# Expert 0's first tile from one-hot products, the index behind it, and what is moved around them

## The chip, the core and the metric

One core of a Trainium2 chip runs one program. The metric is the device time of one execution in microseconds (us); the kernel before took 702.99 us (median of 3 runs, 701.35 to 705.62). Engines: PE (TensorE, matmul), with PEld for its weight loads; DVE (VectorE); ACT (ScalarE); POOL (GpSimd); SP (SyncE, which here only issues DMAs). A trailing q, as in ACTq, is the engine's queue: it issues DMAs and reads registers, in order with the engine's own work.

## The reference

Three stages follow one another; each needs all of the one before.

```python
# 1. attention: 4 batches x 8 heads, 576 positions, head size 64, causal window of 64
scores = q @ k.T / 8, masked to 0 <= i - j < 64; attn = softmax(scores); o = attn @ v
x = o as 2304 tokens x 512
# 2. routed experts: 8 experts, 512 -> 1024 -> 512
do_compute = x @ w_skip > 0                      # the other tokens pass through
e = argmax(x @ w_gate); gate = softmax(x @ w_gate)[e]
x[do_compute] += gate * (relu(x @ w1[e]) @ w2[e])
# 3. dense: 512 -> 2048 -> 512
h = x @ w_in; g = h where h >= 1, 0 where h <= -1, else (h + 1)**2 / 4; out = g @ w_out
```

## The kernel before

All in float32, or in pairs of reduced-precision halves (`split`, L130, and `split_pair`, L134: ACT writes the high half, DVE or POOL the rest). The order on every engine is the order of the text; the framework adds only the waits.

**Attention** (L274 to L696) runs over 18 tiles of 128 tokens (NT = 18), software-pipelined: in iteration t come the value product of tile t-3 (`stage_v`), the transposes of t-2 (`stage_t`), the scores of t (`stage_s`), the logits of earlier tiles (`stage_x`, `stage_l`, `stage_l2`) and the routing. Before the first scores, 69 bf16 matmuls (`warm`, L584) run on a constant. Meanwhile SP loads q, k and v and, through `load_raws` (L101), raw expert weights of 512 KB each into 6 buffers, of which `most[0]` may be in use.

**Routing** takes groups of 3 tiles (ROUTES): `route_a` finds each token's expert, `route_b` its rank among that expert's tokens (running counts by matmul), `route_h` makes two one-hot tables and `route_c` multiplies them into a list of token numbers by expert and slot: `acc` for the groups so far, `idx` at the end. `route_g` stores the gates. Groups begin at tiles 0, 3, ..., 15; the last two at t0 = 12 and t1 = 15. Each x tile is stored to the DRAM table `x1` (`store_t`), its gate in column 512.

**Experts** (L699 to L886): expert 0's first tile is gathered from `x1` by `idx` (`fetch(0, 0)`, an indirect DMA issued by POOL), transposed on PE and split (`pre`, `prep`); then `ffn` runs ha, hb, their transposes, and y. `values_load...` (L833) reads the counts of tokens into registers on every engine, ahead of expert 0. Between `fetch(0, 0)` and `pre(0, 0)` stand two weight splits, ACT then DVE; DVE waits in front of its share (`tick_seen`, L824) until POOL has issued the gather. After them ACT issues up to four raw loads (L829). A tile has 128 tokens: experts 2 and 4 have a second one in this run, expert 4 a third, whose gather `fetch(e, 2)` is issued at L866. Within `ffn`, `hooks` place splits, conversions of stage 3's weights (`turn`) and the next expert's preparation.

**Dense stage** (L889 to L1107): 18 tiles in 6 blocks, PE back to back.

`keep_warm(n)` issues n matmuls on constants whose result nobody reads; 14, 20, 80 and 6 of them stand in the end of attention.

Of the kernel before, what the change touches and what calls it, by code (L numbers as in the profile page):

```python
# [13 lines left out]
I32 = mybir.dt.int32  # L14
# [43 lines left out]
WARM = 69  # L58
WARM_COLUMNS = 108
# [3 lines left out]
KEEP = (14, 20, 80, 6, 36)  # L63
PASSES = ((0, 0), (0, 1), (1, 0))
PX_END = {3: "s2", 2: "s1", 1: "s0"}
# [4 lines left out]
def moe_chain(  # L70
# [200 lines left out]
    rawp.append(mctx.enter_context(tc.tile_pool(name="raw1", bufs=RAWS[1])))  # L271


    with ExitStack() as actx:  # L274
# [10 lines left out]
        nc.gpsimd.memset(zero, 0.0)  # L285
        wg_sb = ldp.tile([P, KD, WGW], F32, tag="wg", name="wg_sb", bufs=1)
# [4 lines left out]
        qt = {}  # L291

# [16 lines left out]
        misc = psp.tile([P, 512], F32, tag="misc", name="misc")  # L309
# [10 lines left out]
        def stage_s(t):  # L320


            i, b0 = divmod(2 * t, B)
            m = none if i == 0 else odd if i % 2 else even
            e, o = (i, i - 1) if i % 2 == 0 else (i - 1, i)
            e, o = place[e % 4], place[o % 4]
            s = [psp.tile([P, 4, P], F32, tag=f"s{(2 * t + k) % 3}", name=f"s{2 * t + k}") for k in range(2)]
# [26 lines left out]
        def stage_t(t):  # L354
            last = t + 1 == NT
            if last:
                both = ldp.tile([P, 2, 4, P], F32, tag="q", name="pts_last")
            for k in range(2):
                g = 2 * t + k
                pr = st.pop(("p", g))  # L360
                pt = psp.tile([P, 4, P], F32, tag=f"s{k}" if last else f"pt{k}", name=f"pt{g}")
                for p in range(4):
                    nc.tensor.transpose(pt[:, p, :], pr[:, p, :], ident)
                pts = both[:, k] if last else ap2.tile([P, 4, P], F32, tag="pts", name=f"pts{g}")

                if last or k == 0 or t + 3 == NT:
                    nc.scalar.activation(pts, pt, AF.Copy)
                else:
                    nc.vector.tensor_copy(pts, pt)
                st["pt", g] = pts  # L370

        def stage_v(t):
# [9 lines left out]
            x = ap2.tile([P, H, D], F32, tag="x", name=f"x{t}", bufs=3)  # L382
# [14 lines left out]
            st["x", t] = x.rearrange("p h d -> p (h d)")  # L397
            i, b = divmod(2 * t, B)
# [6 lines left out]
        def stage_x(t):  # L405
            x = st.pop(("x", t))
            px = psp.tile([P, KD, P], F32, tag=PX_END.get(NT - t, f"s{(2 * t + 2) % 3}"), name=f"px{t}")
# [14 lines left out]
        def stage_l(t):  # L422
# [11 lines left out]
            ls = sm.tile([P, P], F32, tag="ls", name=f"ls{t}", bufs=2)  # L434
# [5 lines left out]

        def keep_warm(n):
            spare = psp.tile([P, P], F32, tag="o", name="spare")
            for _ in range(n):
                nc.tensor.matmul(spare, lhsT=ones, rhs=ones, start=True, stop=True)
# [33 lines left out]
        def route_b(t, n, side):  # L478
# [21 lines left out]
            if t + 2 * n < NT:  # L500
                for i in range(n):
                    nc.gpsimd.tensor_tensor(run, run, oh[:, i], ALU.add)
            elif t + n == NT:
                cn = end["rk"][:, 1, 0 : NE + 1]
                for i in range(n):
                    nc.tensor.matmul(cn, lhsT=ones, rhs=oh[:, i], start=(i == 0), stop=False)
                for i in range(n):
                    nc.tensor.matmul(cn, lhsT=ones, rhs=st["oh", t - n][:, i], start=False, stop=False)
                nc.tensor.matmul(cn, lhsT=ones, rhs=run, start=False, stop=True)
                keep_warm(KEEP[1])  # L510
# [3 lines left out]
            nc.vector.tensor_reduce(ps, r2, axis=AX.X, op=ALU.add)  # L514
            rc = sm.tile([P, 2, n], F32, tag="rc", name=f"rc{t}")
# [7 lines left out]
            if t + n == NT:  # L523
                st["cn"] = cn
# [12 lines left out]
        def route_h(t, n, tiles=None):  # L537

            rc = st["rc", t]
            for i in range(n) if tiles is None else tiles:  # L540

                if t + n == NT:
                    eng, also = dve if i == n - 1 else pool, dve
                else:
                    eng = also = dve if t + 2 * n >= NT and i == n - 1 else pool
# [9 lines left out]
        def route_c(t, n):  # L555
# [4 lines left out]
            near = t + 2 * n < NT <= t + 3 * n  # L560
            mid = t + n < NT <= t + 2 * n
            for i in reversed(range(n)):
                to, at = st.pop(("to", t + i))
                nc.tensor.matmul(
                    ix, lhsT=to, rhs=at, start=(not last and not mid and i == n - 1),
                    stop=(not near and not mid and i == 0),
                )
            if last:
                keep_warm(KEEP[2])
            if not near and not mid:  # L570
# [27 lines left out]
        of = {}  # L598
        for j, n in enumerate(ROUTES):
            t0 = len(of)  # L600
            of.update({t0 + i: (t0, i, n, j % 2) for i in range(n)})
        due, since, gates = {}, {}, {}
        for t in range(NT - 1):
# [9 lines left out]
            most[0] = 1 if t < 3 else 2 if t + 4 < NT else RAWS[0] + RAWS[1]  # L613
# [9 lines left out]
            if t >= 5:  # L623
                t0, i, n, side = of[t - 5]
                if i == n - 1:
                    route_a(t0, n)
                    for f, l in (
                        (partial(route_b, t0, n, side), 1),
                        (partial(route_h, t0, n), 1),
                        (partial(route_c, t0, n), 3),  # L630
                    ):
                        due.setdefault(t + l, []).append(f)
                    gates[t + 1] = partial(route_g, t0, n)
# [11 lines left out]
        t1, n = NT - ROUTES[-1], ROUTES[-1]  # L645
        t0 = t1 - ROUTES[-2]
        ranks, later = due.pop(NT - 1), [f for g in sorted(due) for f in due[g]]
        stage_v(NT - 4)
        stage_t(NT - 3)
        stage_s(NT - 1)  # L650
        store_t(NT - 4, nc.sync)
        stage_l2(NT - 6, *of[NT - 6][1:])
        stage_l(NT - 5)
        stage_x(NT - 4)
        stage_v(NT - 3)
        store_t(NT - 3, nc.sync)
        stage_t(NT - 2)
        stage_t(NT - 1)
        ranks[0]()
        stage_v(NT - 2)  # L660
        store_t(NT - 2, nc.sync)
        for f in ranks[1:]:
            f()
        stage_v(NT - 1)
        store_t(NT - 1, nc.sync)
        stage_x(NT - 3)
# [5 lines left out]
        route_a(t0, of[t0][2])  # L672
        end["lg"] = psp.tile([P, 4, P], F32, tag="pt1", name="lg_end")[:, 0, 0 : n * (NE + 1)]
        for f in gates.values():
            f()
# [3 lines left out]
        route_b(t0, *of[t0][2:])  # L679
        route_h(t0, of[t0][2], range(n - 1))  # L680
# [3 lines left out]
        keep_warm(KEEP[3])  # L684
        stage_l2(NT - 1, *of[NT - 1][1:])
        route_g(t0, of[t0][2])
        for f in later:
            f()
# [10 lines left out]
    with ExitStack() as ectx:  # L699
# [3 lines left out]
        def bank(i, shape, name):  # L703
            return psp.tile(shape, F32, tag=f"bank{i}", name=name)
# [25 lines left out]
        def prep(x, name, tag="mxT", into=None):  # L730
            px = bank(3 if tag == "mxT" else 7, [P, KD, P], f"mpx{name}")
            for c in range(KD):
                nc.tensor.transpose(px[:, c, :], x[:, c * P : (c + 1) * P], ident)
# [86 lines left out]
        early_pool.append(ectx.enter_context(tc.tile_pool(name="earlier", bufs=len(EARLY) // 2)))  # L820
        fetch(0, 0)
# [4 lines left out]
        pre(0, 0)  # L826
# [4 lines left out]
        for e in range(1, AHEAD):  # L831
# [3 lines left out]
        for e in range(NE):  # L835
# [9 lines left out]
            def second():  # L845

                xeT[e, 1] = mp.tile([P, 2, KD, P], F32R, tag="mxT", name=f"mxT{e}_1")
                with tc.If(counts[e] > P):
                    prep(xe[e, 1], f"{e}_1", "mxTl", xeT[e, 1])

# [4 lines left out]
                    work(turn if e else [], [dve]),  # L855
# [9 lines left out]
            with tc.If(counts[e] > P):  # L865
                fetch(e, 2)  # L866
# [22 lines left out]
    with ExitStack() as fctx:  # L889
# [153 lines left out]
        keep_warm(KEEP[4])  # L1043
# [121 lines left out]
```

## Time and profile before

| | us |
|---|---|
| median of 3 runs | 702.99 |
| the profiled execution | 703.17 |
| its span, first to last instruction | 701.5 |
| attention, to the last value product | 0 to about 97.6 |
| routing of the last tiles, first gather | about 97.6 to 116.5 |
| experts | 116.5 to about 271 |
| dense stage | about 271 to 701.5 |

The span is 1.67 us shorter than the execution's time; that part lies around the program. The prediction is made against 703.17. A time such as "at 103.77" is counted from the span's start. In lines of the timeline the first number is the start, the second the length, "x12" a count of instructions merged into one line, and the bracket at the end tells how long the engine was idle before and what ended that.

### The profile page before, as it was taken

Reading aid. Unit: us, or ns where it says so; the run is one execution under the profiler, and the core shown is the slowest. Engines: PE = TensorE matmul, PEld = TensorE weight load, DVE = VectorE, ACT = ScalarE, POOL = GpSimd, SP = SyncE. Lnnn points to the kernel's source line nnn. Section 1 sums busy time; section 2 is a strip of 40 time slices with the busy share of each in tenths; the row PEclk is TensorE's granted clock in tenths of the full one; section 3 lists DMA queues with packets and bytes.
Section 4 is the critical chain, followed back from the end, with each engine's and each line's share of the span. In section 5 each row is a group of like instructions: output and inputs, shape, how many; then the busy total and the mean of one; then the engine's idle time right before and its main releaser. Section 6 shows DMA issues by size and latency. Waiting matters only on the chain.

```text
span 701.5 us, 12250 instructions
## 1 busy us (share of the span) xinstructions
PE 674.2 (96%) x4630; PEld 575.6 (82%) x4630; DVE 425.6 (61%) x808; ACT 385.9 (55%) x768; POOL 90.7 (13%) x137
## 2 busy tenths in 40 slices
PE   7999989999998998999999999999999999999997
PEld 6777778776776765987989999999999999999995
DVE  4888864897781799787888854444433433433332
ACT  5887742583751764566766655454444454445443
POOL 3255545222210221000000000000000000000000
PEclk9999998999999999999999999999999999999999
DMA  8999953897891693442333202121300030001001
GB/s 259 288 272 290 307 133 115 289 329 275 267 357 31 205 332 95 172 127 84 121 92 96 69 0 61 31 60 31 91 1 0 1 91 0 1 1 45 1 1 45
DMA packets 34504, 88.83 MB, mean 127 GB/s; under 512 B 6958, under 2 KB 8110, under 8 KB 34420
## 3 DMA queue, kind: packets, MB, share of 16 engines
q1 hardware_dynamic: 26208, 73.82, 34.3%
q10 hardware_dynamic: 5892, 7.35, 3.1%
q0 software_dynamic: 2320, 6.58, 2.8%
q8 instruction: 48, 0.79, 0.5%
q14 instruction: 36, 0.29, 0.1%
HBM read 75.65 MB, written 13.12 MB: 127 GB/s over the span
## 4 chain that ended last, share of the span: by engine, by line
PE 55%; DVE 3%; ACT 1%; issue 1%; ACTq 0%; DVEq 0%
PE h L922 27%; PE po L950 26%; PE spare L1038 1%; PE p2x L912 1%; DVE c L943 1%; DVE c L940 1%; ACT q L933 1%; DVE w L137 1%; DVE gs L941 0%; DVE q L932 0%; DVE x2T L132 0%; ACT q L929 0%; DVE q L936 0%; ACT part L959 0%; ACT w L136 0%
## 5 line engine op out<-in xcount | busy, mean ns | idle before, releaser
L922 PE MATMUL h<-x2T,w 128*128 128x384 f32 x1152 | 218.0, 337 | 1.1 <-DVE x2T L132 0.9
L950 PE MATMUL po<-w,gs 128*128 128x512 f32 x864 | 217.3, 395 | 1.7 <-ACT w L136 0.9
L922 PEld LDWEIGHTS h<-x2T,w 128*128 128x128 f32 x1152 | 204.6, 188 | 10.0 <-DVE x2T L132 1.7
L950 PEld LDWEIGHTS po<-w,gs 128*128 128x128 f32 x864 | 159.5, 188 | 32.3 <-ACT w L136 1.2
L929 ACT ACTIVATE q<-h 128x384 f32<-128x384 f32 x96 | 47.0, 489 | 108.1 <-PE h L922 104.2
L932 DVE TENSOR_SCALAR q<-q 128x384 f32<-128x384 f32 x96 | 34.4, 358 | 98.2 <-ACT q L929 98.0
L936 DVE TENSOR_TENSOR q<-hs,q 128x384 f32<-128x384 f32 x96 | 53.7, 559 | 49.8 <-ACT q L933 49.8
L938 ACT ACTIVATE gs<-q 128x384 fp32r<-128x384 f32 x96 | 50.4, 525 | 60.0 <-DVE q L936 60.0
L941 DVE TENSOR_TENSOR gs<-q,gs 128x384 fp32r<-128x384 f32 x96 | 53.6, 559 | 44.4 <-ACT gs L938 44.4
L136 ACT ACTIVATE w<-raw 128x1024 fp32r<-128x1024 f32 x64 | 65.3, 1056 | 18.7 <-PEq L869 4.7
L798 PE MATMUL y<-w,hT 128*128 128x512 f32 x264 | 70.2, 403 | 4.1 <-DVE hT L132 2.8
L137 DVE TENSOR_TENSOR w<-raw,w 128x1024 fp32r<-128x1024 f32 x55 | 64.8, 1219 | 3.8 <-ACT w L136 1.9
L933 ACT ACTIVATE q<-q 128x384 f32<-128x384 f32 x96 | 50.5, 526 | 22.2 <-DVE q L932 18.6
L798 PEld LDWEIGHTS y<-w,hT 128*128 128x128 f32 x264 | 47.3, 188 | 17.3 <-DVE hT L132 4.5
L349 ACT ACTIVATE pr<-s,nb 128x128 f32<-128x128 f32 x144 | 39.2, 384 | 16.5 <-DVE nb L345 16.5
L931 ACT ACTIVATE hs<-h 128x384 f32<-128x384 f32 x96 | 46.7, 487 | 0.0
L759 PE MATMUL ha<-w,mxT 128*128 128x512 f32 x132 | 35.3, 416 | 3.7 <-ACT mxT L131 1.5
L759 PEld LDWEIGHTS ha<-w,mxT 128*128 128x128 f32 x132 | 25.1, 197 | 13.2 <-issue 4.5
L759 PE MATMUL hb<-w,mxT 128*128 128x512 f32 x132 | 35.2, 402 | 0.0
L345 DVE TENSOR_REDUCE nb<-s 128x4 f32<-128x512 f32 x36 | 23.2, 686 | 16.0 <-PE s L338 14.5
L724 POOL DMA_INDIRECT x<-mx,idx x11 | 16.5, 1501 | 115.6 <-POOLq L865 60.4
L131 ACT ACTIVATE hT<-hTp 128x512 fp32r<-128x512 f32 x22 | 13.2, 599 | 27.1 <-PE hTp L772 13.0
(170 smaller groups left out, 702.1 us busy)
## 6 DMA issues: line engine op xcount, KB each, us to landing
raw<-in_wu SPq DMA_DIRECT2D x61, 512.0 KB, 6.0
raw<-in_wd SPq DMA_DIRECT2D x31, 512.0 KB, 4.0
x<-x SPq DMA_DIRECT2D x22, 256.0 KB, 3.2
vt<-in_vs SPq DMA_DIRECT2D x36, 130.0 KB, 6.2
out<-out SPq DMA_DIRECT2D x36, 128.0 KB, 2.4
x<-x ACTq DMA_DIRECT2D x17, 256.0 KB, 6.6
q<-in_qs SPq DMA_DIRECT2D x8, 512.0 KB, 5.0
kt<-in_ks SPq DMA_DIRECT2D x8, 512.0 KB, 6.2
```

Of the source, the lines that this page charges most:

```text
L136: nc.scalar.activation(t[:, 0], src, AF.Copy)
L137: eng.tensor_tensor(t[:, 1], src, t[:, 0].bitcast(F32), ALU.subtract)
L759: nc.tensor.matmul(ph, lhsT=xT[:, a, c, :], rhs=halves[4 * e + j, c][:, b, :], start=(n == 0), stop=(n == len(seq) - 1),)
L798: nc.tensor.matmul(py, lhsT=hT[j][:, a, c, :], rhs=halves[4 * e + 2 + j, c][:, b, :], start=(j == 0 and n == 0), stop=(j == 1 and n == len ...
L922: nc.tensor.matmul(ph, lhsT=halves[U_IN + m // 4, c][:, b, (m % 4) * P : (m % 4 + 1) * P], rhs=xT[:, a, c, :], start=(n == 0), stop=(n == ...
L929: nc.scalar.activation(q, ph, AF.Relu, bias=0.5, scale=0.5)
L931: nc.scalar.activation(h, ph, AF.Copy)
L933: nc.scalar.activation(q, q, AF.Square)
L936: nc.vector.tensor_tensor(q, h, q, ALU.max)
L938: nc.scalar.activation(gs[:, 0], q, AF.Copy)
L941: dve.tensor_tensor(gs[:, 1], q, gs[:, 0].bitcast(F32), ALU.subtract)
L950: nc.tensor.matmul(po[i], lhsT=gs[:, a, i * P : (i + 1) * P], rhs=w[:, b, :], start=(m == m0 and (a, b) == PASSES[0]), stop=(m == m1 - 1 a ...
```

## The change

- The 69 matmuls at the start become 6: float32, 512 columns, on a tile `warmer` that DVE fills with ones after its other constants.
- The four `keep_warm` calls in the end of attention go.
- At most 2 raw buffers are filled at t = 14 (6 before), 3 at t = 15 and 16, and 6 from a new `load_raws()` on, behind `stage_v(NT - 3)`.
- x of tiles 12 to 17 stays in SBUF (`xs_late`; 12 to 14 in parts of k's buffer that are no longer used).
- The group of tiles 9 to 11 is ranked earlier and added to `acc`; `gather_ahead` then fetches the rows of expert 0's first tile that lie in tiles 0 to 11 into `rows`, which POOL has cleared.
- `choose` makes for each late tile a one-hot matrix from rank to slot (tiles 12 to 14 by two activations on ACT, 15 to 17 by one operation on DVE), and `add_rows` multiplies the tile with it: six tiles and `rows` (against the identity) add up in PSUM to the transposed tile that `prep` splits.
- `route_h` and `route_c` of the last groups, so `idx` and `cnt_i`, come behind these products; the gates of the last two groups behind `route_a`, those of tiles 9 to 11 much earlier.
- The gathers of expert 1 and then expert 0 are issued ahead of `tick_seen`; those behind it are expert 0's second tile and expert 2's first.
- `fetch(e, 2)` moves into the middle of the expert's first tile (it stood behind that tile's store).
- An expert that has one conversion in `turn` does it in hook 2, not in hook "a".

```diff
-WARM = 69
-WARM_COLUMNS = 108
+WARM = 6
-KEEP = (14, 20, 80, 6, 36)
+KEEP = 36
...
+        warmer = ap2.tile([P, 4, P], F32, tag="pr", name="warmer", bufs=4)
+        nc.vector.memset(warmer, 1.0)
...
+        def choose(t, i, eng):
+            sel = kept(*SEL_AT[t + i - t0], P)
+            ps = st["ps", t][:, i : i + 1]
+            if eng is nc.scalar:
+                off = sm.tile([P, P], F32, tag="ls", name=f"off{t + i}", bufs=3)
+                nc.scalar.activation(off, slot_r[:, 0], AF.Abs, bias=ps)
+                nc.scalar.activation(sel, off, AF.Relu, bias=1.0, scale=-1.0)
+            else:
+                eng.tensor_scalar(sel, slot_r[:, 0], ps, 0.0, op0=ALU.add, op1=ALU.is_equal)
+            return sel
+        def gather_ahead():
+            at = sm.tile([P, 1], I32, tag="ahead", name="ahead", bufs=1)
+            nc.vector.tensor_copy(at, acc[:, 0:1])
+            nc.gpsimd.indirect_dma_start(
+                out=rows, out_offset=None, in_=x1[0 : t0 * P], in_offset=bass.IndirectOffsetOnAxis(ap=at, axis=0),
+                bounds_check=t0 * P - 1, oob_is_err=False,
+            )
+        def add_rows(px, x, sel, first=False, last=False):
+            for c in range(KD):
+                nc.tensor.matmul(
+                    px[:, c, :], lhsT=x[:, c * P : (c + 1) * P], rhs=sel,
+                    start=(first and c == 0), stop=(last and c == KD - 1),
+                )
...
-        warm = psp.tile([P, P], F32, tag="o", name="warm")
+        warm = psp.tile([P, H, P], F32, tag="o", name="warm")[:, 0:4]
         for _ in range(WARM):
-            nc.tensor.matmul(warm[:, 0:WARM_COLUMNS], lhsT=ones, rhs=ones[:, 0:WARM_COLUMNS], start=True, stop=True)
+            nc.tensor.matmul(warm, lhsT=warmer[:, 0], rhs=warmer, start=True, stop=True)
...
-            most[0] = 1 if t < 3 else 2 if t + 4 < NT else RAWS[0] + RAWS[1]
+            most[0] = 1 if t < 3 else 2 if t + 3 < NT else 3
...
+        x0 = bank("s0", "mpx0_0")
+        sels = [choose(t0, 0, nc.scalar)]
+        add_rows(x0, xs_late[t0], sels[0], first=True)
         route_a(t1, n)
-        route_h(t0, of[t0][2], [n - 1])
+        route_p(t0, n0)
+        route_h(t0, n0, range(n0 - 1))
+        sels += [choose(t0, i, nc.scalar) for i in range(1, n0)]
+        route_g(t0, n0)
         route_g(t1, n)
-        keep_warm(KEEP[0])
         route_b(t1, *of[t1][2:])
-        route_h(t1, n)
-        route_c(t0, of[t0][2])
+        for i in range(1, n0):
+            add_rows(x0, xs_late[t0 + i], sels[i])
+        add_rows(x0, rows, ident)
+        sels += [choose(t1, i, dve) for i in range(n)]
+        for i in range(n):
+            add_rows(x0, xs_late[t1 + i], sels[n0 + i], last=(i == n - 1))
+        route_h(t0, n0, [n0 - 1], dve)
+        route_p(t1, n)
+        route_h(t1, n, [0])
+        route_h(t1, n, range(1, n), dve)
+        route_c(t0, n0)
         route_c(t1, n)
...
+        xeT[0, 0] = prep(None, "0_0", px=x0)
+        fetch(1, 0)
         fetch(0, 0)
...
         work(splits, [dve] * 2)
-        pre(0, 0)
...
-        for e in range(1, AHEAD):
+        for e in range(2, AHEAD):
             fetch(e, 0)
...
                     prep(xe[e, 1], f"{e}_1", "mxTl", xeT[e, 1])
+                    fetch(e, 2)
...
-                    work(turn if e else [], [dve]),
+                    work(turn if len(turn) > 1 else [], [dve]),
```

## Rows read from the trace of the kernel before

**Rows 1.** Page, part 1: busy us, share of the span, instructions.

```profile
PE 674.2 (96%) x4630; PEld 575.6 (82%) x4630; DVE 425.6 (61%) x808; ACT 385.9 (55%) x768; POOL 90.7 (13%) x137
```

**Rows 2.** Waits of PE, 5 to 98 us: total us, times, longest us.

```profile
PE o L388 <- DMA vt<-in_vs: 2.2, 4, 1.3
PE s L329 <- ACT pr L349: 1.6, 1, 1.6
```

**Rows 3.** Timeline of the start.

```profile
1.12 6.21 PE L586 MATMUL warm<-ones 128*128 128x108 bf16 x69 [1.12 <-DVE ones L199]
4.84 0.91 DVE L288 MEMSET kt<- 128x1024 f32 x1
7.69 0.86 PEld L338 LDWEIGHTS s<-kt,q 64*64 64x64 f32 x32 [0.42 <-ACT q L591]
```

**Rows 4.** Instructions of lines 586, 338, 388: duration ns min/median/max, first and last start.

```profile
L586 PE MATMUL warm<-ones x69: 211/296/296, 1.1 to 7.1; 128*128 128x108 bf16 x69
L338 PE MATMUL s<-kt,q x576: 269/269/321, 7.7 to 89.9; 64*64 64x128 f32 x192
L388 PE MATMUL o<-vt,pts x544: 219/222/271, 15.7 to 95.4; 128*64 128x65 f32 x182
```

**Rows 5.** SP's waits, 0 to 120 us: total us, times, longest us.

```profile
SPq L305 <- DMA raw<-in_wu: 2.3, 1, 2.3
```

**Rows 6.** Timeline from the last logits to expert 0's first transposes.

```profile
101.66 0.38 ACTq L533 DMA_DIRECT2D x<-gate  x1
103.77 0.54 PE L449 MATMUL lg_end<-quarters,ls 128*128 128x9 f32 x2
106.36 0.23 PE L484 MATMUL rk_end<-oh,stri 128*128 128x27 bf16 x1
110.24 0.16 DVE L573 TENSOR_TENSOR cnt_i<-rk_end,base 128x9 int32<-128x9 f32 x1
111.22 1.23 POOL L715 DMA_INDIRECT mx<-x,idx  x1 [1.88 <-DVE cnt_i L573]
112.65 2.34 DVE L137 TENSOR_TENSOR w<-raw,w 128x1024 fp32r<-128x1024 f32 x2
112.75 3.06 POOL L715 DMA_INDIRECT mx<-x,idx  x1 [0.18 <-issue]
116.53 3.05 PE L759 MATMUL ha<-w,mxT 128*128 128x512 f32 x12 [0.81 <-ACT mxT L131]
117.29 0.70 ACTq L115 DMA_DIRECT2D raw<-in_wu  x1
120.82 0.60 PE L772 MATMUL hTp<-ident,h 128*128 128x128 f32 x4
```

**Rows 7.** Prices: instructions of lines (ns), timeline, gathers' landing, lines by form (busy us, mean ns).

```profile
L547 DVE TENSOR_SCALAR to<-slot_r,rc x2: 281/296/311, 105.7 to 108.4; 128x128 fp32r<-128x128 f32 x2
...
65.40 1.09 PE L363 MATMUL pt<-ident,pr 128*128 128x128 f32 x8
...
DMA to landing us min/median/max: 3.7/7.2/9.1
...
L833 PEldq TENSOR_LOAD <-cnt_i x1: 780/780/780, 115.1 to 115.1; - x1
...
L349 ACT ACTIVATE pr<-s,nb 128x128 f32<-128x128 f32 x144 | 39.2, 384 | 16.5 <-DVE nb L345 16.5
```

**Rows 8.** Stretches: PE, PEld, DVE, ACT, POOL busy, granted clock, DMA share, GB/s.

```profile
102.00:103.00 1.00, 0.59 (x4) 0.59 (x5) 0.66 (x5) 0.52 (x3) 0.38 (x1) 0.78 0.20 2
...
109.00:110.00 1.00, 1.00 (x11) 1.00 (x11) 0.00 (x0) 0.03 (x1) 0.33 (x2) 0.80 0.00 0
```

**Rows 9.** Timeline of expert 4's third tile.

```profile
213.19 0.63 PE L733 MATMUL mpx<-ident,mx 128*128 128x128 f32 x4 [1.75 <-DMA mx<-x,idx]
214.50 4.60 PE L759 MATMUL ha<-w,mxT 128*128 128x512 f32 x12 [0.69 <-ACT mxT L131]
```

**Rows 10.** Timeline of expert 6.

```profile
254.66 1.19 PE L798 MATMUL y<-w,hT 128*128 128x512 f32 x4 [0.60 <-DVE hT L132]
```

More of the change, by code (lines that the diff above doesn't have):

```diff
@@ L291, in moe_chain, with kept @@
         qt = {}
+        def kept(s, lo, n):
+            return kt[:, s].rearrange("p b q k -> p (b q k)")[:, lo : lo + n]
         def load_q(i):
@@ L308, in moe_chain, with bank @@
         end = {}
-        misc = psp.tile([P, 512], F32, tag="misc", name="misc")
+        def bank(tag, name):
+            return (pxp if tag == "s0" else psp).tile([P, 4, P], F32, tag=tag, name=name)
         def corner(col, side, n):
@@ L326, in stage_s @@
             e, o = place[e % 4], place[o % 4]
-            s = [psp.tile([P, 4, P], F32, tag=f"s{(2 * t + k) % 3}", name=f"s{2 * t + k}") for k in range(2)]
+            s = [bank(f"s{(2 * t + k) % 3}", f"s{2 * t + k}") for k in range(2)]
             for k in range(2):
@@ L360, in stage_t @@
                 pr = st.pop(("p", g))
-                pt = psp.tile([P, 4, P], F32, tag=f"s{k}" if last else f"pt{k}", name=f"pt{g}")
+                pt = bank(f"s{k}" if last else f"pt{k}", f"pt{g}")
                 for p in range(4):
@@ L433, in stage_l @@
                 )
-            ls = sm.tile([P, P], F32, tag="ls", name=f"ls{t}", bufs=2)
+            ls = sm.tile([P, P], F32, tag="ls", name=f"ls{t}", bufs=3)
             if t + 3 >= NT:
@@ L439, in stage_l @@
             st["ls", t] = ls
[L441 to L444, printed above, removed]
         def stage_l2(t, i, n, side):
@@ L559, in route_c @@
             last = t + n == NT
-            near = t + 2 * n < NT <= t + 3 * n
             mid = t + n < NT <= t + 2 * n
-            for i in reversed(range(n)):
+            for i in range(n):
                 to, at = st.pop(("to", t + i))
                 nc.tensor.matmul(
-                    ix, lhsT=to, rhs=at, start=(not last and not mid and i == n - 1),
-                    stop=(not near and not mid and i == 0),
-                )
-            if last:
-                keep_warm(KEEP[2])
-            if not near and not mid:
+                    ix, lhsT=to, rhs=at, start=(not last and i == 0), stop=(not mid and i == n - 1),
+                )
+            if not mid:
                 nc.vector.tensor_tensor(idx if last else acc, ix, acc, ALU.add)
@@ L649, in moe_chain @@
         stage_t(NT - 3)
+        for f in gates.values():
+            f()
         stage_s(NT - 1)
+        rows = kept(*ROWS_AT, RW)
+        nc.gpsimd.memset(rows, 0.0)
+        ranks[0]()
         store_t(NT - 4, nc.sync)
@@ L654, in moe_chain @@
         stage_x(NT - 4)
+        for f in ranks[1:]:
+            f()
         stage_v(NT - 3)
+        most[0] = RAWS[0] + RAWS[1]
+        load_raws()
         store_t(NT - 3, nc.sync)
@@ L658, in moe_chain @@
         stage_t(NT - 1)
-        ranks[0]()
         stage_v(NT - 2)
         store_t(NT - 2, nc.sync)
-        for f in ranks[1:]:
-            f()
         stage_v(NT - 1)
         store_t(NT - 1, nc.sync)
+        for f in later:
+            f()
+        gather_ahead()
         stage_x(NT - 3)
@@ L671, in moe_chain @@
         stage_l2(NT - 4, *of[NT - 4][1:])
[L672 to L675, printed above, removed]
+        n0, n = ROUTES[-2:]
+        route_a(t0, n0)
         stage_l(NT - 3)
@@ L678, in moe_chain @@
         stage_l(NT - 1)
-        route_b(t0, *of[t0][2:])
-        route_h(t0, of[t0][2], range(n - 1))
+        end["lg"] = psp.tile([P, 4, P], F32, tag="pt1", name="lg_end")[:, 0, 0 : n * (NE + 1)]
         end["rk"] = psp.tile([P, 4, P], F32, tag="s2", name="rk_end")
@@ L703, in bank @@
         def bank(i, shape, name):
+            if i == 3:
+                return pxp.tile(shape, F32, tag="s0", name=name)
             return psp.tile(shape, F32, tag=f"bank{i}", name=name)
@@ L728, in store_x, with prep @@
             apart(dma, "scatters", ("scatters", "gathers"))
[L730 to L733, printed above, removed]
+        def prep(x, name, tag="mxT", into=None, px=None):
+            if px is None:
+                px = bank(3 if tag == "mxT" else 7, [P, KD, P], f"mpx{name}")
+                for c in range(KD):
+                    nc.tensor.transpose(px[:, c, :], x[:, c * P : (c + 1) * P], ident)
             if into:
```

62 lines of the change are left out of this document (35 added, 27 removed).

## The prediction

> **What bounds the kernel.** I read the page first: PE is busy for 96% of the span [rows 1], so the question at every place is whether PE's own order sets the pace. Then the waits of PE in attention: in 93 us it waits 2.2 us for v and 1.6 us once, early, for an exponential [rows 2]. So attention is paced by PE, and what delays its first scores delays its end. Then the timeline between attention and the experts, where PE runs matmuls nobody reads while a chain of small steps goes on [rows 6]. Last, the waits inside the experts [rows 9, 10]. The dense stage is PE back to back and the change leaves it alone: whatever is won or lost by 271 us stays.
>
> **Start: +5.5 us (3.1 to 8.0).** Before, the 69 bf16 matmuls end at 7.3, just ahead of the first scores at 7.69, which wait 0.42 us for q [rows 3]. Now six float32 matmuls stand there, on a tile that DVE fills where it used to begin clearing k at 4.84. 1024 elements took 0.91 us, so 512 take about 0.46, and PE starts at about 5.36.
>
> Each float32 matmul is two instructions in the trace (576 of L338 for 288 in the source). One of 128 columns lasts 269 ns, one of 65 columns 219 [rows 4]: 50 ns for 63 columns, 0.79 ns a column, which is an estimate from these two lines. Twelve instructions of 512 columns are 4.9 us at this rate, 9.7 at half of it. Which rate? The 69 before started 90 ns apart, 108 columns at 1.2 GHz; their duration is 296 ns but for the last ones at 211 [rows 3, 4], so PE came to the higher level only near 7.1, six us after its first matmul. I take 5 us at the low level: 6.2 instructions, then 5.8 at 0.41 us, an end at 12.7, first scores at about 13.2 (0.5 us of mask product in between) against 7.69. The bounds are the higher level from the first instruction (10.75, +3.1) and the lower for all (15.6, +8.0). Nothing hides it: q, k and v land meanwhile, but PE waits for none of them until 85 us.
>
> **Raw loads: -1.5 us (-2.2 to 0).** The load of v that PE waits for at 85 us, up to 1.3 us at once [rows 2], stood on SP behind a raw load, which cost SP 2.3 us [rows 5]. With 2 or 3 raw buffers instead of 6 it leaves on time, and the longest wait and the one behind it go, 1.5 of the 2.2 us. The other 0.7 us are for the last block's v, whose load follows directly on the product that frees its buffer. The three raw loads moved there stand behind it on SP, ahead of the stores of tiles 15 to 17, by at most 0.7 us each (the slowest issue of rows 6); those stores have over 10 us until a gather needs them. The four rank operations of tiles 9 to 11, now ahead of DVE's copies, cost DVE about 4 x 0.17 us (as small as the one at 110.24, 0.16 [rows 6]): 0.7 us, which fall into that same wait for v and would cost as much without it.
>
> **From the last value product to expert 0: 0 us (-3.6 to +5.6).** I keep the times of before here, as if attention ended where it did.
>
> The logits of the last tile wait behind ACT, which issues a gate store at 101.66 once DVE has the gate [rows 6]; that store is now long done. So the last logits end near 103.0 instead of 104.3, and PE ranks the last group from 104.9 instead of 106.3 [rows 6]. The one-hots of tiles 12 to 14 are six activations on ACT, each at most 0.38 us [rows 7], done by 105.3, behind the rank; those of 15 to 17 are three at 0.30 us on DVE [rows 7], done by 106.9, behind the products of the others. Late, they would cost PE their 0.7 or 0.3 us a tile.
>
> PE has 7 x 4 = 28 products, so 56 instructions of 128 columns. No row shows this one; the nearest are float32 transposes, 8 in 1.09 us with 0.28 us for the last to finish, 0.116 us apart [rows 7], so 0.23 a product and 6.4 us together. Four run ahead of the rank; the other 24 take 5.5 us, from 105.1 to 110.6. `rows` is asked for near 99 and gathers land after 3.7 to 9.1 us [rows 7], so it is there for its turn at 107 or late by 1 us. Before, the transposed tile stood 0.81 us ahead of ha, at 115.7 [rows 6]: 5.1 us are won.
>
> But `idx` and `cnt_i` now come behind it, at about 112.1 instead of 110.4: six list products (0.9 at the pace of the transposes) and DVE (0.5). PE reads the counts into registers ahead of expert 0, 0.78 us [rows 7], formerly hidden under the gather. So ha starts at about 113.0, not when its input is ready, against 116.53 [rows 6]: 3.5 us.
>
> And that is not the end of it. POOL issues two gathers (1.25 us each) before DVE may go on: 114.7 instead of 112.5. Then two splits of DVE, 2.34 us [rows 6], end at 117.1 instead of 115.0. ACT's third and fourth raw load need the buffers that these free; the fourth is issued at about 118.0, as before [rows 6]. Behind them in ACT's queue stand its own register read (0.8) and the evacuation of ha: PE transposes ha at about 119.5 against 120.82 [rows 6], after 2 us of idling. Only 1.3 us of the 3.5 are left.
>
> The clock takes the rest. Before, it fell from 2.4 to 1.2 GHz at 102.6, after a thin stretch of small products, and came back near 109.4, behind dense matmuls [rows 8]. That thin stretch stays, and the matmuls that filled gaps are gone; the products are dense from about 105 on. I take 2.6 us of work at half the pace, +1.3. In sum 0. The lower bound is the full 3.6, the upper 28 products at the low level throughout, +6.9 on -1.3.
>
> **Experts: -3.3 us (-3.9 to 0).** Expert 4's third tile waits 1.75 us for its gather, the clock falls, and its ha takes 4.60 us against expert 0's 3.05 [rows 9, 6]. With the gather issued about a tile earlier the 1.75 us go. Of the 1.55 I count 1.05: PE still idles 0.7 us or more there for the split. So -2.8. In expert 6 PE waits 0.60 us for DVE's half of hT [rows 10], which stood behind a conversion that now comes later: -0.5. The same move for experts 1 and 5 hides behind PE, which did not wait there; if DVE ran late it would cost what the conversion does, 2.5 us.
>
> **Sum.** 5.5 - 1.5 + 0 - 3.3 = +0.7, on the profiled execution's 703.17 (0.18 above the median shown): **703.9 us**, no change that a measurement of this kernel can tell, which takes about 1%, or 7 us.
>
> **Rivals.**
> 1. *The start costs nothing.* Then -4.8: 698.4. It would need the six products to be done by 7.7, 2.3 us after their tile exists; 0.79 ns a column speaks against it, unless they stream at one cycle a column at the high level at once (2.6 us).
> 2. *The hand-over does not hold ACT*, since the raw loads find other buffers or DVE is let go earlier: PE transposes ha at 117.3, -3.5 instead of -1.3, with no loss of clock: 700.4. With rival 1 it would be 694.9. For it: ha's input is ready early. Against it: the order on POOL, DVE and ACT above.
> 3. *The clock stays down* from 103 through the products and expert 0's first 18 matmuls. That is +6.9 for products and lists and, past the idling ahead of ha's transposes, about 2.5 for ha and hb, instead of +1.3: 712.0. For it: with filler matmuls it took from 102.6 to 109.4 to return [rows 8]. Against it: float32 products are dense. It decides if the low level lasts past 110. The Trainium skill (TensorE: Matmul & The Clock Gate, "Why this matters for your kernels") has the rule this rival rests on: gaps between bursts of matmuls bring the slower clock back. The fall at 102.6 agrees; by that rule the change, which takes 120 filler matmuls out, would be slower by this rival's sum.
> 4. *The third tile wins nothing*, its clock falling all the same and another wait in place of the gather's: 706.7.
>
> **Chances.** Forecast 0.52, rival 1 0.14, rival 2 0.10, rival 3 0.14, rival 4 0.10. Below 696 lie about 0.10 of rival 1 (with a part of rival 2) and 0.03 of rival 2: faster 0.13. Above 710 lie 0.11 of rival 3 and 0.02 of the forecast with the start at its upper bound: slower 0.13. Same 0.74. The range runs from the start's lower bound with both gains in full (3.1 - 2.2 - 1.3 - 3.9 = -4.3, and a little of rival 1 below it: 698) to its upper bound with the clock lost for a while (8.0 - 1.5 + 1.5 - 1.6 = +6.4: 710).
>
> **What the profile after would show.** First scores at 12 to 14 us, six wide products before them at first some 0.8 us an instruction; no PE wait for v near 85 plus the shift; the last value product about 4 us later than 97.6; 56 product instructions in about 6.4 us if the clock holds; ha starting 0.8 us behind `cnt_i`; ACT reaching ha late, with PE idle about 2 us ahead of its transposes; no wait for the gather in expert 4's third tile. It would be wrong if the first scores start near 8, if ACT takes ha as soon as PE is done, or if the granted clock is 0.5 past 110 plus the shift.

## The result and the profile after

The changed kernel takes 710.14 us (median of 20 runs, 707.76 to 712.12) against 703.17 for the kernel before, measured beside it. The ratio is 1.0088, 95% interval 1.0068 to 1.0109: slower by a little under 1%, within what the prediction called no change, but at the very end of its range (698 to 710) and 6.2 us above its 703.9. One of the 20 runs of the kernel before took 939.47 us; the others lie between 700.15 and 709.51, and the median hardly moves without it. The profiled execution took 710.3 us with a span of 708.6; it is compared with the 703.17 and 701.5 of before.

Page of the changed kernel, part 1 (the same part of the page of before is [rows 1]): PE has 125 matmuls fewer, is busy 3.3 us less, and yet the span is 7.1 us longer. So the time is in waits, not in work.

```profile
PE 670.9 (95%) x4505; PEld 567.1 (80%) x4505; DVE 427.5 (60%) x814; ACT 387.3 (55%) x774; POOL 92.3 (13%) x139
```

Timeline of its start [rows 3]. The weight loads show the pace of the twelve wide instructions: 0.85 us apart up to 10.55, then 0.43, so the higher of the two clock levels came near 10.8 us, 5.5 us after the first. (The granted clock in the profile reads 1.00 from the start, since its record begins only at 10.75; the level before that is read from the pace.) The first scores start at 13.76 against 7.69.

```profile
4.73 0.48 DVE L291 MEMSET warmer<- 128x512 f32 x1
5.27 8.12 PE L622 MATMUL warm<-warmer 128*128 128x512 f32 x12 [5.27 <-DVE warmer L291]
...
8.85 0.34 PEld L622 LDWEIGHTS warm<-warmer 128*128 128x128 f32 x1 [0.52 <-issue]
9.70 0.34 PEld L622 LDWEIGHTS warm<-warmer 128*128 128x128 f32 x1 [0.52 <-issue]
...
11.52 0.19 PEld L622 LDWEIGHTS warm<-warmer 128*128 128x128 f32 x1 [0.24 <-issue]
11.94 0.19 PEld L622 LDWEIGHTS warm<-warmer 128*128 128x128 f32 x1 [0.24 <-issue]
...
13.76 1.10 PE L349 MATMUL s<-kt,q 64*64 64x128 f32 x32
```

Waits of PE in the changed kernel, 5 to 110 us [rows 2]: the wait for v has not gone, and two waits for DVE are new.

```profile
PE o L402 <- DMA vt<-in_vs: 1.8, 3, 0.9
...
PE misc L460 <- DVE r L522: 1.3, 1, 1.3
...
PE misc L446 <- DVE acc L607: 0.5, 1, 0.5
```

Timeline from the last value product to the transposes of ha [rows 6]. The 56 product instructions of L565 come in four groups, with a wait for the first one-hot (1.11 us) and for `rows` (0.57); ha 1.35 us behind the end of `cnt_i`; and then ACT, which evacuates ha only at 126.19, behind the fourth raw load, itself behind DVE's two splits.

```profile
103.27 1.12 PE L402 MATMUL o<-vt,pts_last 128*64 128x65 f32 x30 [0.69 <-DMA vt<-in_vs]
...
110.58 1.16 PE L565 MATMUL mpx<-kt 128*128 128x128 f32 x8 [1.11 <-ACT kt L549]
...
111.93 2.03 PE L565 MATMUL mpx<-kt 128*128 128x128 f32 x16
...
114.54 1.16 PE L565 MATMUL mpx<-ident,kt 128*128 128x128 f32 x8 [0.57 <-DMA kt<-x,ahead]
...
115.53 2.84 PE L565 MATMUL mpx<-kt,x 128*128 128x128 f32 x24
...
119.27 0.16 DVE L609 TENSOR_TENSOR cnt_i<-rk_end,base 128x9 int32<-128x9 f32 x1
...
120.78 3.01 PE L816 MATMUL ha<-w,mxT 128*128 128x512 f32 x12 [1.77 <-DVE mxT L135]
...
122.62 2.34 DVE L140 TENSOR_TENSOR w<-raw,w 128x1024 fp32r<-128x1024 f32 x2
...
124.99 0.33 ACTq L118 DMA_DIRECT2D raw<-in_wu  x1
...
126.19 0.60 ACT L823 ACTIVATE h<-ha 128x512 f32<-128x512 f32 x1 [5.16 <-issue]
...
126.84 0.66 PE L829 MATMUL hTp<-ident,h 128*128 128x128 f32 x4 [1.69 <-ACT h L823]
```

Timeline of expert 4's third tile [rows 9]: no wait for the gather, and ha at full pace, 3.06 us against 4.60.

```profile
219.12 0.60 PE L790 MATMUL mpx<-ident,mx 128*128 128x128 f32 x4
220.41 3.06 PE L816 MATMUL ha<-w,mxT 128*128 128x512 f32 x12 [0.69 <-ACT mxT L134]
```

Waits of PE in the experts, 130 to 300 us, columns as in the waits above: y now waits for ACT's half of hT, three times.

```profile
PE y L855 <- ACT hT L134: 4.4, 3, 1.6
```

Timeline of expert 6, where one of the three stands [rows 10]. The conversion of expert 5 (L170, begun at 249.40; its last operation stands here) now runs on DVE when expert 6 has begun. Behind it come y's addition for expert 5 and DVE's way past the jump (DVEq L924), for which ACT waits 3.22 us; so ACT does not get to hT before 253.17.

```profile
251.64 0.69 DVE L170 SCALAR_TENSOR_TENSOR c<-raw,c 128x512 f32<-128x512 f32 x1
252.25 0.74 DVE L860 SCALAR_TENSOR_TENSOR mx<-y,mx 128x512 f32<-128x512 f32 x1
253.17 0.60 ACT L134 ACTIVATE hT<-hTp 128x512 fp32r<-128x512 f32 x1 [3.22 <-DVEq L924]
...
253.82 1.65 PE L855 MATMUL y<-w,hT 128*128 128x512 f32 x6 [1.37 <-ACT hT L134]
```

Laid side by side, by the lag of the changed kernel's trace behind that of before: +6.07 at the first scores; +6.74 at the last value product; +6.02 at ha's transposes; +7.89 at expert 2's second tile; +4.38 at expert 5, behind the third tile; +6.16 at the dense stage's filler; +7.10 at its first transposes, where PE waits 0.78 us for x. From there on it stays.

### The profile page after: what moved, and what is told of

Same layout as the page of the kernel before. It is cut to its first block, busy times and chain, and to the rows that moved or that the text cites. A ratio compares the mean times of both kernels' runs of the same rounds, so it can differ in the third digit from the quotient of the medians.

```text
span 708.6 us, 12028 instructions
## 1 busy us (share of the span) xinstructions
PE 670.9 (95%) x4505; PEld 567.1 (80%) x4505; DVE 427.5 (60%) x814; ACT 387.3 (55%) x774; POOL 92.3 (13%) x139
## 4 chain that ended last, share of the span: by engine, by line
PE 50%; DVE 7%; ACT 2%; issue 1%; DMA 1%; ACTq 0%; SPq 0%; DVEq 0%
PE po L1008 24%; PE h L980 24%; DVE c L1001 2%; ACT q L991 1%; PE p2x L970 1%; DVE gs L999 1%; DVE c L998 1%; DVE w L140 1%; DVE c_first L1107 1%; DVE q L990 1%; DVE q L994 1%; DMA x<-x 1%; DVE x2T L135 0%; ACT q L987 0%; PE spare L1096 0%
## 5 line engine op out<-in xcount | busy, mean ns | idle before, releaser
L816 PE MATMUL ha<-w,mxT 128*128 128x512 f32 x132 | 33.4, 399 | 4.8 <-DVE mxT L135 2.5
L356 DVE TENSOR_REDUCE nb<-s 128x4 f32<-128x512 f32 x36 | 23.2, 686 | 20.5 <-PE s L349 18.9
```

Source lines behind the costliest of these rows:

```text
L816: nc.tensor.matmul(ph, lhsT=xT[:, a, c, :], rhs=halves[4 * e + j, c][:, b, :], start=(n == 0), stop=(n == len(seq) - 1),)
```

## The experiments

The traces give two theories to test: that the start is worth its 6 us to the end, and that the moved conversions eat what the third tile wins. Four kernels on one chip, beside 703.82 us for the kernel before.

**The old start in the changed kernel.**

```diff
-WARM = 6
+WARM = 69
+WARM_COLUMNS = 108
...
         for _ in range(WARM):
-            nc.tensor.matmul(warm, lhsT=warmer[:, 0], rhs=warmer, start=True, stop=True)
+            nc.tensor.matmul(warm[:, 0:WARM_COLUMNS], lhsT=ones, rhs=ones[:, 0:WARM_COLUMNS], start=True, stop=True)
```

> The changed kernel with the 69 bf16 matmuls of the kernel before at its start. Theory (PE paces attention, so the 6.07 us by which the first scores came later reach the end in full): 704.1 us, 6.0 less than the changed kernel's 710.1, with the first scores near 7.7 us; the wait for v that the changed kernel has near 36 us (0.93 and 0.18 us) should be gone too if it hangs on how the loads fall against the late start, which would make it 702.6. Rival (attention waits for its loads, so a later start costs less than it is long): 707 to 710, with more waits for v in its place.

Measured 712.95 us, ratio to before 1.0131 (1.0084 to 1.0178): both expectations missed. The last value product started at 96.30 us instead of 103.27, so attention did gain its 7 us. They were lost again in the experts, in waits that neither original kernel has (PE, 130 to 300 us):

```profile
PE ha L815 <- PEq L923: 8.7, 4, 4.1
...
PE ha L815 <- PEq L930: 1.2, 1, 1.2
PE ha L815 <- ACTq L923: 1.2, 1, 1.2
```

L923 is the `tc.If` around an expert's second tile. PE idles there when the expert has none and the program jumps over that tile. L930 is the one around a fourth tile, which expert 4 does not have.

**The new start in the kernel before.**

```diff
-WARM = 69
-WARM_COLUMNS = 108
+WARM = 6
...
-            nc.tensor.matmul(warm[:, 0:WARM_COLUMNS], lhsT=ones, rhs=ones[:, 0:WARM_COLUMNS], start=True, stop=True)
+            nc.tensor.matmul(warm, lhsT=warmer[:, 0], rhs=warmer, start=True, stop=True)
```

> The kernel before with one edit of the change: six float32 matmuls on a tile that DVE fills, in place of the 69. Theory: 709.2 us, 6.07 more than 703.2, or 710.7 if the changed kernel's extra wait for v near 36 us comes from the late start too. Rival (the late start gives the loads time, so a part of the 6 us comes back in the waits for v near 85 us): 705 to 708.

Measured 724.95 us, ratio 1.0307 (1.0255 to 1.0360): 21 us slower, from six matmuls. The same waits in the same stretch (there L866 is the `tc.If` around the second tile, L874 the one around the fourth):

```profile
PE ha L760 <- PEq L866: 13.3, 4, 3.8
...
PE ha L760 <- PEq L874: 1.3, 1, 1.3
PE ha L760 <- ACTq L866: 1.2, 1, 1.2
```

What the two runs share is that PE has 57 matmuls more or fewer than the kernel that was edited, so 114 instructions with the weight loads, and that all its later code stands 114 instructions further on or back. The two original kernels differ by 125 matmuls [rows 1], 250 instructions. (Counted are matmuls and weight loads alone.) Two runs further down test the position alone.

**The single conversions back in hook "a".**

```diff
-                    work(turn if len(turn) > 1 else [], [dve]),
+                    work(turn if e else [], [dve]),
```

> The changed kernel with the single conversions of experts 1, 5 and 6 back in hook a. Theory (the moved conversion stands on DVE at the next expert's start, in front of the subtraction that ACT's next splits and its half of hT wait for; in the traces experts 2, 6 and 7 lost 1.87, 0.85 and 0.99 us): 706.4 us, 3.7 less than 710.1, with no wait of over 1 us of y for ACT's hT. Rival (these waits come from raw loads that now arrive later, and not from the conversion): 710, with the waits of y for hT still there.

Measured 706.34 us, ratio 1.0039 (1.0012 to 1.0067), so 3.4 to 3.8 us less than the changed kernel by ratio and by median. The waits of y for ACT's hT fell from 4.4 us to this, and in experts 2, 6 and 7 its trace falls behind that of before by 0.07, 0.28 and 0.00 us, where the changed kernel's fell behind by 1.87, 0.85 and 0.99:

```profile
PE y L855 <- ACT hT L134: 0.4, 1, 0.4
```

**Only the third tile's gather earlier, in the kernel before.**

```diff
                     prep(xe[e, 1], f"{e}_1", "mxTl", xeT[e, 1])
+                    fetch(e, 2)
...
             with tc.If(counts[e] > P):
-                fetch(e, 2)
                 tile_of(e, 1)
```

> The kernel before with one edit of the change: the third tile's gather is issued in the middle of the expert's first tile. Theory (the wait of 1.75 us for the gather and the slower ha behind it go): 699.7 us, 3.4 less than 703.2, with expert 4's third tile 3.4 us earlier against its second. Rival (the wait moves on to another input, such as the split): 702 to 703.

Measured 699.47 us, ratio 0.9943 (0.9910 to 0.9975). One line of the change, alone, makes the kernel faster. Its trace at the third tile, without the 1.75 us of [rows 9]:

```profile
210.60 0.60 PE L733 MATMUL mpx<-ident,mx 128*128 128x128 f32 x4
211.88 2.37 PE L759 MATMUL ha<-w,mxT 128*128 128x512 f32 x9 [0.69 <-ACT mxT L131]
```

Four more kernels, beside 703.31 us for the kernel before.

**An early start of as many PE instructions as the changed kernel's.** Twelve bf16 matmuls of 512 columns on the constant that is there from 1.1 us on.

```diff
-WARM = 6
+WARM = 12
...
-            nc.tensor.matmul(warm, lhsT=warmer[:, 0], rhs=warmer, start=True, stop=True)
+            nc.tensor.matmul(
+                warm, lhsT=ones, rhs=ones.rearrange("p (o k) -> p o k", o=1).to_broadcast([P, 4, P]),
+                start=True, stop=True,
+            )
```

> The changed kernel with 12 bf16 matmuls of 512 columns on the constant, from about 1.1 us, in place of the six float32 ones on the filled tile: the same number of PE instructions, so that all later code stands where it stood. In the two runs that moved PE's code by 114 instructions (the old start in the changed kernel, the new start in the kernel before) PE idled 3.8 to 4.1 us at the jumps past a second tile. Theory (PE paces attention; where the code stands decides the wait at the jumps): 704.1 us, first scores near 7.5, no such wait at the jumps. Rival (the waits at the jumps come from the earlier start itself, through loads or splits): 712, as with the old start.

Measured 705.65 us, ratio 1.0031 (1.0005 to 1.0057). The longest wait of PE at a jump is 0.4 us, as in the changed kernel. (The 3.8 to 4.1 us that the expectation names are the longest of the waits at the jumps; the shortest were 1.2.) The scores begin 7.8 us earlier, but attention's last value product only 4.5: PE now waits for its loads (below, under the hardware).

**The new start in the kernel before, its PE instructions made up to the old number.** 57 bf16 matmuls of one column while PE would idle for the tile of ones.

```diff
-WARM = 69
-WARM_COLUMNS = 108
+WARM = 6
+PAD = 57
...
+        for _ in range(PAD):
+            nc.tensor.matmul(warm[:, 0, 0:1], lhsT=ones, rhs=ones[:, 0:1], start=True, stop=True)
         for _ in range(WARM):
...
+            nc.tensor.matmul(warm, lhsT=warmer[:, 0], rhs=warmer, start=True, stop=True)
```

> The kernel before with the new start, and ahead of it 57 bf16 matmuls of one column in PE's idle time from 1.1 to 5.3 us, so that PE has as many instructions as the kernel before. Theory (the 21 us of the run without them are 6.1 of start and some 15 of waits at the jumps, from where the code stands): 709.3 us, the waits at the jumps gone. Rival (the late start itself brings those waits): 724, as without them.

Measured 708.34 us, ratio 1.0055 (1.0028 to 1.0082), 16.6 us less than without the 57, whose work lies in idle time. The waits at the jumps are back to what they were:

```profile
PE ha L763 <- PEq L873: 0.4, 1, 0.4
PE ha L763 <- PEq L877: 0.4, 1, 0.4
```

So where the code stands decides, not when it runs. (The 57 also bring the first scores forward, to 12.81 from 13.73, but by the last value product, at 101.50 and 101.56, nothing is left of that.) The start itself costs the kernel before 5.0 us by the medians, 3.9 by the ratio.

**Raw loads around expert 0 on SP.**

```diff
-        load_raws(nc.scalar)
+        load_raws()
         fetch(0, 1)
...
-        load_raws(nc.scalar)
+        load_raws()
         for e in range(NE):
```

> The changed kernel with the raw loads around expert 0's start issued by SP instead of ACT. Theory (ACT, in order, holds the evacuation of expert 0's ha behind two loads that wait for DVE's splits): ACT takes ha near 124.4 instead of 126.2 after the start of the span, PE waits no longer for it, 708.3 us. Rival (DVE's splits, which end at 125, are late next and hold hT and so y): 709.5 to 710.1.

Measured 706.66 us, ratio 1.0058 (1.0037 to 1.0079). Its timeline: ACT takes ha 3.0 us after ha's start (5.4 before the edit), while SP's next two raw loads still wait for DVE.

```profile
120.03 2.97 PE L816 MATMUL ha<-w,mxT 128*128 128x512 f32 x12 [1.79 <-DVE mxT L135]
...
123.04 0.60 ACT L823 ACTIVATE h<-ha 128x512 f32<-128x512 f32 x1 [2.78 <-PE ha L816]
123.09 0.33 SPq L121 DMA_DIRECT2D raw<-in_wd  x1
124.21 0.60 PE L829 MATMUL hTp<-ident,h 128*128 128x128 f32 x4
```

From ha's start to expert 1's it is 13.63 us instead of 15.58: 1.95 us, as expected, and DVE does not take them back. By ratio the edit is worth 2.1 us; by the medians, which were measured at different times, 3.5, more than the trace explains.

**The ranks of tiles 9 to 11 ahead of the last scores.**

```diff
+        ranks[0]()
+        stage_s(NT - 1)
         for f in gates.values():
             f()
-        stage_s(NT - 1)
...
-        ranks[0]()
         store_t(NT - 4, nc.sync)
```

> The changed kernel with the ranks of tiles 9 to 11 ahead of the last scores, and the gate operations behind them. Theory (PE's wait of 1.3 us for the rank product's reader r stands behind DVE's two maxima of the last scores): that wait goes, the last value product starts about 1.1 us earlier, 709.0 us. Rival (the maxima then come later and the last exponentials hold PE by as much): 709.8 to 710.5, with a wait for the exponentials or for r's one-hot in its place.

Measured 709.05 us, ratio 1.0084 (1.0054 to 1.0114): by time alone not told apart from the changed kernel. The trace shows the wait gone (PE's product of L460 ahead of DVE's maxima of L356; in the changed kernel r stood behind them):

```profile
93.86 0.39 PE L460 MATMUL misc<-quarters,ls 128*128 128x9 f32 x2
94.04 1.29 DVE L356 TENSOR_REDUCE nb<-s 128x4 f32<-128x512 f32 x2
```

Against the run before it, which has the same code up to there, the distance from the scores of t = 16 to the last value product is 1.2 us shorter.

Three more kernels, beside 703.27 us for the kernel before.

**All four together**: the early start, the conversions back, the raw loads on SP and the early ranks.

> The changed kernel with the four edits that each won alone: 12 bf16 matmuls of 512 columns at the start (-4.5 us measured), the single conversions back in hook a (-3.8), the raw loads around expert 0 on SP (-3.5, of which the traces explain 1.95), the ranks of tiles 9 to 11 ahead of the last scores (-1.1). Theory (they lie in four stages, one after the other, and PE sets the pace in each, so they add up): 710.1 - 4.5 - 3.8 - 1.95 - 1.1 = 698.8 us. Rival (a load or DVE takes up what PE is let go, as v did for a part of the earlier start): 700 to 703.

Measured 697.62 us, ratio 0.9920 (0.9891 to 0.9950): faster than both kernels, the four gains adding up.

**The same with the counts read later**, within expert 0's first tile.

```diff
-        _, counts = nc.values_load_multi_w_load_instructions(cnt_i[0:1, 0:NE], min_val=0, max_val=N)
+        counts = []
+        def read_counts():
+            counts.extend(nc.values_load_multi_w_load_instructions(cnt_i[0:1, 0:NE], min_val=0, max_val=N)[1])
...
                 "a": lambda: (
+                    None if counts else read_counts(),
```

> The same with the counts read into registers within expert 0's first tile, behind the transposes of ha, where PE waits for the split anyway. Theory (ha of expert 0 starts only when PE has read the counts, some 0.8 us after its input is ready): 698.0 us, ha 0.8 us sooner. Rival (ha waits for DVE's half of its input, which ends no earlier than the counts): 698.8.

Measured 698.88 us, ratio 0.9925 (0.9897 to 0.9953). ha starts 1.3 us after the last product instead of 2.4, as the theory has it, but the total can't be told from the run without it. Inconclusive for the time.

**Two edits of the change in the kernel before**: the third tile's gather, as above, and the rule for raw loads.

```diff
-            most[0] = 1 if t < 3 else 2 if t + 4 < NT else RAWS[0] + RAWS[1]
+            most[0] = 1 if t < 3 else 2 if t + 3 < NT else 3
...
         stage_v(NT - 3)
+        most[0] = RAWS[0] + RAWS[1]
+        load_raws()
...
```

> The kernel before with two edits of the change: the third tile's gather earlier (699.5 us measured alone) and at most 2 or 3 raw buffers filled until the last block's v is asked for. Theory (the raw load on SP ahead of v made PE wait for v at 85 us; in the runs with the change's rule the score iteration there is 4.8 to 5.1 us long and not 6.8): 697.7 us, no wait for v of over 0.5 us near 85. Rival (the waits for v come from how busy the transfers are, not from SP's order): 699.5.

Measured 699.04 us, ratio 0.9932 (0.9908 to 0.9957); the gather alone gave 0.9943, so the raw rule's gain is not measured by the time. In the trace the scores of t = 16 and 17 stand 4.84 us apart, 6.74 before, and no wait for v is left between them; that execution lost 0.93 us to a wait for v near 36 us.

## Why the prediction was right, and where its sum was not

The time came out as forecast in that it changed by under 1%, but only just; the sum came out 6.4 us low: +7.1 instead of +0.7.

**Start, +5.5: right, +6.07.** The step held as worked out: 0.85 us an instruction at the lower level, 0.43 at the higher, the rise 5.5 us after the first. What it did not see is that the number of these matmuls has a second effect, through the place of the code behind them, of 7 to 17 us at other numbers (712.95 us for the old start against 705.65 for the early start of the right length; 724.95 against 708.34 with the 57). At the change's own number, 250 instructions fewer in all, the waits at the jumps are as small as before. That is luck: with another number of warm-up matmuls or products the forecast would have missed by that much.

**Raw loads, -1.5: right where it was said, and not seen in the sum.** The wait near 85 is gone in the changed kernel and in the old-start run (4.84 and 4.83 us between the scores of the last two tiles, 6.74 before), 1.9 us. In the kernel before with the late start it does not go (5.77 us there, and 6.71 with the 57), so it is not the late start that removes it. But the profiled execution has a wait for v near 36 us that moved the lag by 1.45. Three runs whose code is the same up to there (conversions back, raw loads on SP, ranks early) don't have it; one of the kernel before with the raw rule, which differs from before only from t = 14 on, does: it comes in some executions and is no effect of the change.

**The four rank operations, "0.7 us, which fall into that same wait for v": wrong, +1.3.** I summed DVE's work and not its order: r stands behind the two maxima of the last scores (1.29 us), and PE's next product into the same PSUM tile waits for r. Moving it showed 1.2 us. The sum of the tiles' list into `acc`, moved likewise, holds PE for 0.5 us more.

**Last value product to expert 0, 0: -0.7 in the trace.** Here the mechanism was right in its main part. The products kept PE busy for 7.0 us instead of 6.4 and waited twice; ha came 1.35 us after `cnt_i` instead of 0.9 and was 2.5 us earlier instead of 3.5, counted from the last value product; ACT, held by the raw loads, gave back all but 0.7 of it. Taking the loads off ACT gave 1.95 us, which is rival 2 in the size of that step, made true by an edit. The clock term (+1.3) did not occur in the profiled execution, but in others with the same products: there the way from the last value product to ha takes 18.15 to 19.77 us against 17.51, so 0.6 to 2.3 more, and as a mean the term was fair. Windows of 4 us (busy PE, PEld, DVE, ACT, POOL, clock, DMA share, GB/s), first the changed kernel, then the run with the conversions back, whose code is the same up to there:

```profile
108.00:112.00 4.00, 2.86 (x49) 2.43 (x41) 2.83 (x19) 2.78 (x11) 0.70 (x2) 1.00 0.80 252
112.00:116.00 4.00, 3.42 (x32) 3.23 (x30) 3.04 (x13) 0.00 (x0) 3.83 (x6) 1.00 0.12 5
116.00:120.00 4.00, 3.00 (x28) 2.85 (x26) 0.94 (x3) 1.46 (x3) 0.00 (x0) 1.00 0.09 12
```

```profile
108.00:112.00 4.00, 2.86 (x32) 2.44 (x25) 2.84 (x19) 2.77 (x11) 0.70 (x2) 0.79 0.67 210
112.00:116.00 4.00, 4.00 (x32) 3.94 (x31) 2.73 (x13) 0.00 (x0) 2.96 (x5) 0.50 0.10 1
116.00:120.00 4.00, 4.00 (x32) 4.00 (x32) 0.23 (x1) 0.00 (x0) 0.82 (x2) 0.86 0.00 0
```

The first took 17.51 us from the last value product to ha, the second 19.77: 2.3 us for the fall, with ha at 4.56 instead of 3.01 us on top. Seven of the eight traces with the products show a clock below 1.00 among them, so rival 3 has the fall right more often than not; a low level that lasts without a break from 103 us through expert 0's first 18 matmuls none of them shows. The rule of the Trainium skill that the rival names (TensorE: Matmul & The Clock Gate, "Why this matters for your kernels") has gaps between bursts of matmuls bring the slower clock back. With it agree these seven traces, with 0.50 for 4 us in the one above; the eighth, with much the same gaps and 1.00 throughout, shows that gaps do not decide it alone. No run puts the 120 filler matmuls back, so what their removal costs is not shown.

**Experts, -3.3: the step that failed.** The third tile won 3.4 us (I had taken 2.8), and alone it makes the kernel before 0.57% faster. The moves of the single conversions were the error: "hides behind PE, which did not wait there". PE did not wait there because the conversion ended before the next expert began. Later by half a tile it stands in front of y's addition, and behind that addition ACT's and DVE's next work waits: +1.87, +0.85 and +0.99 us in experts 2, 6 and 7, 3.7 in all, and undoing it won 3.4 to 3.8. The prediction even gave the price, "if DVE ran late it would cost what the conversion does, 2.5 us", but expected a gain of 0.5 in expert 6 where there was a loss, let the term's bounds end at 0, and at the upper end of the whole range still counted on 1.6 us of gain. The last 0.9 us are at the dense stage's first transposes, which wait 0.78 us for x; they wait 0.7 us with the conversions back too, and in executions of the kernel before with the earlier gather 0.3 and, with the raw rule as well, 1.2; why x is late there stays open.

In sum: 6.07 at the start, 0.67 in the rest of attention, -0.72 up to ha's transposes, 0.14 in the experts (3.7 - 3.4 and small), 0.94 ahead of the dense stage: 7.1.

In the chances one step does not hold: 0.10 of rival 1's 0.14 was put below 696, although that rival's own time is 698.4.

**What the one-hot products are worth** stays small even with ACT let go: from the last value product to expert 1 the kernel with all four edits took 33.5 us, 32.4 with the counts read later, the changed kernel with the raw loads on SP 31.8, and the kernel before with the two edits 33.1. The clock alone moves such a stretch by as much as these differ. The totals of the first two and the last, 697.6, 698.9 and 699.0, have overlapping intervals. No run has the products without the rest of the change, so their own worth is argued from these stretches and not measured.

## What to carry to other kernels

An operation that hides where it stands need not hide half a tile later: before pricing a move at nothing, name what stands behind it on its engine at the new place, and who waits for that. An experiment that adds or removes instructions ahead of a jump must keep their number, or it measures the place of the code as well: here 57 matmuls of one column made 16.6 us of difference. And where a change bundles many edits, try each alone: one line of this one won 0.57%, and the rest lost more than that.

## What the runs showed of the hardware

- **A jump's cost depends on where the code stands.** With PE's code moved by 114 instructions, PE idles 1.2 to 4.1 us at each of five jumps over a second tile and 1.2 to 1.3 at the one over a fourth (11.1 us in all with the old start in the changed kernel, 15.8 with the new start in the kernel before); with the count restored, 0.4 us each at most. The Trainium skill (Runtime: NRT & Kernel Launch, "Instruction fetch mechanics") says that instructions are fetched in blocks of 256, in sequence, and that a taken branch to a block that isn't there has to wait for a fetch. The traces agree, with waits of up to 4.1 us. As an estimate from the Trainium skill's block of 256, the 250 instructions between the two kernels would be nearly one block, and 114 nearly half of one. The traces also show transfers that fit a fetch: DMA queue 8, of the kind "instruction", moves 16 KB at a time (48 packets, 0.79 MB; the line is from the page of the new start in the kernel before). In that run's three waits of 3.7 to 3.8 us, which end at 152.29, 254.81 and 273.95, such a transfer begins 1.1 to 1.3 us after PE has fallen idle and lasts 1.0 to 1.1, and PE goes on 1.5 to 1.6 us after its end. That the queue is PE's is inferred from this. Which positions are good was tried at these points only and stays open.

```profile
q8 instruction: 48, 0.79, 0.5%
```

- **An early start makes attention wait for its loads, by how much differs from one execution to the next.** Two runs with the same start and the same code up to t = 16 began their scores at 5.99 and 6.09 us and reached those of t = 16 at 84.61 and 82.66. Waits of PE, 5 to 88 us, first the early start alone, then all four edits:

```profile
PE s L338 <- ACT pr L358: 2.9, 2, 1.6
PE o L400 <- DMA vt<-in_vs: 1.9, 3, 0.8
PE o L400 <- issue: 0.8, 1, 0.8
PE s L347 <- DMA kt<-in_ks: 0.3, 1, 0.3
```

```profile
PE s L338 <- ACT pr L358: 3.1, 2, 1.7
...
```

The second wait for an exponential (`pr`) in each goes back to a load too: ACT, in order, had to scale q first, and q was late. In the run with all four edits it waited 2.56 us for q, and PE then 1.35 us, until 22.18, for the exponential:

```profile
20.05 1.06 ACT L327 ACTIVATE q<-q 128x1024 f32<-128x1024 f32 x1 [2.56 <-DMA q<-in_qs]
```

- **The granted clock is not a property of the code alone.** In the same stretch of the same instructions it was 1.00 throughout in one execution and 0.50 for 4 us in another. What decides it was not found. A clock term taken from one profile is worth an expectation, not a sum.
